# Routing attention and a mixture of experts: first tiles of three experts run ahead, while the last sequence's tokens are placed

## Chip, core and metric

The kernel runs on one core of a Trainium2 chip. The metric is the device time of one execution in microseconds. Before the change the median of three runs is 895.67 us (895.34 to 895.93).

## What is computed

Attention over 4 sequences, 8 heads, 768 positions and 64 channels, in which a query sees only keys of its own cluster of 16, and then a mixture of 8 experts over the 3072 rows of 512 that come out, each row through the one expert that its gate chooses:

```
q_assign, k_assign = argmax(q_n . c_n), argmax(k_n . c_n)
scores = where(q_assign == k_assign, scale * q @ k.T, -1e9)
x = softmax(scores) @ v                       # rows: batch x position, 8 heads side by side
expert_idx = argmax(x @ w_gate)
y[row] = relu(x[row] @ w1[e]) @ w2[e]         # e = expert_idx[row]; w1 512 x 1024, w2 1024 x 512
out = gate_weight * y
```

## The kernel before

**Attention.** Heads are taken in pairs: 16 groups, four to a sequence. A group has 12 units (two halves of the queries by six blocks of keys), and the loop goes in turns of three units, four turns to a group. In each turn `score` makes three score tiles (PSUM tile `sps`, L418 and L421) and their exponentials on ACT (`A`, L423), DVE adds these up (`T`, L426 and L430), and `attend` multiplies the turn before by `v` (`O`, L438). All else is a list of jobs, each set by hand to a turn and to the part of it ahead of or behind `attend`: the turning of q and k for the next group (L344), clusters and their one-hots (`similar`, `assign`, `put`; L358 to L401), `weigh` and `weigh2` (denominators and gate logits, L456 to L489), `x_turn` (rows of x back to tokens, L499 and L502), `gate`, and `keep_rows`, which writes a sequence's rows to `x_rows` in DRAM (L523). The score tiles have three buffers of two PSUM banks (`sps`), the output one bank (`O`), and all the small products one bank with a single buffer (`mps`).

**Placing.** When attention is done, the tokens of all four sequences are placed at once, in an order that a scheduler makes. A scan on DVE ranks the tokens of each partition per expert (`pr`, L613), two small matmuls count across partitions (`cps`, L618), and each token gets a slot: 416 slots for each expert (three tiles of 128 and one of 32), and beyond that a place in spare tiles. To turn slots into lists of tokens, DVE makes one-hots of a slot's row and column (`oh_r`, `oh_c`), POOL multiplies `oh_c` by the token's number (L690), and 24 fp32 matmuls add up `tok_ps` (L698). From it DVE makes the index lists `g_idx` and `s_idx`.

**Experts.** A group is an expert's four tiles, or one spare tile (two of these are always run, further ones in a loop that this data does not enter). `gather` fetches rows by indirect DMAs on POOL (`xg`, L724), `turn_rows` turns them on TensorE and DVE (`tp`, `xgT`, L734 and L735), `layer1` makes 8 blocks of hidden units (`hp`, L743) with the ReLU by turns on DVE (L748) and ACT (L750), `layer2` makes the output tiles (`zp`, L781; the 32-row tile as four quarters, `zq`, and a fold), and `rows_out` scales and scatters them (`zo`, L754; L755). The loop over groups is in written order: layer 1 of a group, turn of the next, layer 2, gather of the one after, fetch of the weights three ahead. Weights have three buffers; those of experts 0 to 2 are fetched during attention, 4 MB each.

PSUM in this stage is laid out anew: three banks for `hp`, two for `tp`, two for `zp`, one for `zq`.

Of the kernel before, what the change touches and what calls it, by code (L numbers as in the profile page):

```python
# [20 lines left out]
NB = 3  # L21
XU = 2
RQ = 32


def in_general(tc, ident, ident_b, first_c, first_e, wpool, q, k, v, centroids, w_gate, w1, w2, out):
# [13 lines left out]
    with tc.tile_pool(name="gen", bufs=1) as sb, tc.tile_pool(name="gen_ps", bufs=1, space=PSUM) as pp:  # L40
# [88 lines left out]
        with tc.For_i(0, N // P, 1) as i:  # L129
# [26 lines left out]
            for e in range(E):  # L156
                we1 = wpool.tile([P, DB, F], F32, name="w1")
                we2 = wpool.tile([P, FB, Dm], F32, name="w2")
# [24 lines left out]
def kernel(  # L183
# [33 lines left out]
    NX = -(-(N - CAP) // P)  # L217
# [7 lines left out]
    wpool = ctx.enter_context(tc.tile_pool(name="weights", bufs=3))  # L225

    def fetch(e):
        w1 = wpool.tile([P, DB, F], F32, name="w1")
        w2 = wpool.tile([P, FB, Dm], F32, name="w2")
        nc.sync.dma_start(out=w1, in_=moe_w1[bass.ds(e, 1)].rearrange("e (a p) f -> p (e a) f", p=P))  # L230
        nc.sync.dma_start(out=w2, in_=moe_w2[bass.ds(e, 1)].rearrange("e (a p) d -> p (e a) d", p=P))
        return w1, w2
# [18 lines left out]

    with ExitStack() as actx:
# [9 lines left out]
        ps_s = actx.enter_context(tc.tile_pool(name="ps_s", bufs=NB, space=PSUM))  # L262
        ps_o = actx.enter_context(tc.tile_pool(name="ps_o", bufs=1, space=PSUM))
        ps_m = actx.enter_context(tc.tile_pool(name="ps_m", bufs=1, space=PSUM))
        actx.enter_context(tc.manual_schedule())
# [35 lines left out]
        ohs = []  # L301
        for i in range(2):
            t = consts.tile([P, 2 * NQ, 2, D], BF16, name=f"oh{i}")
            nc.gpsimd.memset(t, 0.0)
            ohs.append(t)
# [76 lines left out]
        def assign2(g):  # L382
            rank = sims.pop(g)
            top = asg.tile([P, G], F32, name="top")
            nc.vector.tensor_reduce(top, rank, axis=AX, op=ALU.max)
            nc.vector.tensor_tensor(
                ohs[g % 2][:, :, :, 0:C], rank.rearrange("p (t a) c -> p t a c", a=2),
                top.rearrange("p (t a) -> p t a", a=2).unsqueeze(3).to_broadcast([P, 2 * NQ, 2, C]), op=ALU.is_equal,
            )

        def put(g):
            ohT[g] = ohp.tile([P, 2, S], BF16, name="ohT")
            ps = ps_s.tile([P, 2, 512], F32, name="sps").bitcast(BF16)
            for w in range(2):
                for j in range(NQ):
                    nc.tensor.transpose(  # L396
                        ps[:, w, j * P : (j + 1) * P],
                        ohs[g % 2][:, (j % (NQ // 2)) * 4 + w * 2 + j // (NQ // 2)].rearrange("p a c -> p (a c)"), ident_b,
# [92 lines left out]
        def x_turn(g, half):  # L491
# [4 lines left out]
            ps = ps_m.tile([P, 512], F32, name="mps")  # L496
# [41 lines left out]
        NTURN = NG * TG  # L538
        for g in range(NG):
# [10 lines left out]
            at(n + TG + 2, 0, weigh, g)  # L550
            at(n + TG + 2, 1, weigh2, g)
            at(n + TG + 3, 1, x_turn, g, 0)
            at(n + TG + 4, 0, x_turn, g, 1)
            if g % HP == HP - 1:
                at(n + TG + 3, 0, gate, g // HP)
                at(n + TG + 4, 0, keep_rows, g // HP)
# [3 lines left out]
        def early(e):  # L560
            weights[e] = fetch(e)

        for e in range(3):
            at(HP * TG * (e + 1) - 7, 0, early, e)
# [14 lines left out]
    lt_strict = consts.tile([P, P], F32)  # L579
    nc.gpsimd.memset(lt_strict, 1.0)  # L580
    nc.gpsimd.affine_select(
        lt_strict, lt_strict, compare_op=ALU.is_gt, fill=0.0, base=0, pattern=[[1, P]], channel_multiplier=-1,
    )
    ones_sq = consts.tile([P, P], F32)
    nc.gpsimd.memset(ones_sq, 1.0)
    zero_e = consts.tile([P, E], F32)
    nc.gpsimd.memset(zero_e, 0.0)
    keep = consts.tile([P, E, NT], F32)
    nc.gpsimd.memset(keep, 1.0)
    nc.gpsimd.memset(keep[:, :, 0:1], 0.0)  # L590
    b1off = iota("b1off", [P, E], [[(NJ + 1) * P, E]], -1, 0)
    b2off = iota("b2off", [P, E], [[-(NJ + 1) * P, E]], E * (NJ + 1) * P - CAP, 0)
    thr = iota("thr", [P, NX], [[P, NX]], CAP, 0)
    kx = iota("kx", [1, NX], [[1, NX]], 0, 0)
    iota_f = iota("iota_f", [P, P], [[1, P]], 0, 0)
    tokv = iota("tokv", [P, B, NQ], [[S, B], [1, NQ]], 1, NQ)

    g_idx = rte.tile([P, NC], I32)
    s_idx = rte.tile([P, NC], I32)
    xe = rte.tile([1, NX + 2], I32)  # L600

    with tc.tile_pool(name="sm", bufs=1) as sm, tc.tile_pool(name="rps", bufs=1, space=PSUM) as rps:
        sc = sm.tile([P, NT, E], F32)
        nc.vector.tensor_tensor(sc, lg, lmax.unsqueeze(2).to_broadcast([P, NT, E]), op=ALU.is_ge)
        nc.vector.tensor_tensor(sc, sc, first_e[:, None, :].to_broadcast([P, NT, E]), op=ALU.mult)
        mx2 = sm.tile([P, NT], F32)
        nc.vector.reduce_max(mx2, sc, axis=AX)
        sel = sm.tile([P, E, NT], F32)
        nc.vector.tensor_tensor(
            sel.rearrange("p e t -> p t e"), sc, mx2.unsqueeze(2).to_broadcast([P, NT, E]), op=ALU.is_equal,  # L610
        )
        pr = sm.tile([P, E, NT], F32)
        nc.vector.tensor_tensor_scan(  # L613
            pr.rearrange("p e t -> p (e t)"), keep.rearrange("p e t -> p (e t)"), sel.rearrange("p e t -> p (e t)"),
            0.0, op0=ALU.mult, op1=ALU.add,
        )
        cps = rps.tile([P, 2, E], F32, name="cps")
        nc.tensor.matmul(cps[:, 0, :], lhsT=lt_strict, rhs=pr[:, :, NT - 1], start=True, stop=True)  # L618
        nc.tensor.matmul(cps[:, 1, :], lhsT=ones_sq, rhs=pr[:, :, NT - 1], start=True, stop=True)
        cnt = sm.tile([P, 2, E], F32)  # L620
        nc.vector.tensor_copy(cnt, cps)
# [3 lines left out]
            og, cnt[:, 1, :].unsqueeze(2).to_broadcast([P, E, NX]), thr[:, None, :].to_broadcast([P, E, NX]),  # L625
            op=ALU.is_gt,
# [7 lines left out]
        nc.vector.scalar_tensor_tensor(b2, in0=b2, scalar=float(P), in1=b2off, op0=ALU.mult, op1=ALU.add)  # L634
        xk = sm.tile([1, NX, E], F32)
        nc.vector.tensor_tensor(
            xk, ove[0:1, None, :].to_broadcast([1, NX, E]), kx[0:1, :].unsqueeze(2).to_broadcast([1, NX, E]),
            op=ALU.is_le,
        )

# [6 lines left out]
        bps = rps.tile([P, 1], F32, name="bps")  # L647
# [12 lines left out]
        slot = sm.tile([P, E, NT], F32)  # L660
        nc.vector.tensor_tensor(slot, pr, cnt[:, 0, :].unsqueeze(2).to_broadcast([P, E, NT]), op=ALU.add)
        gx = sm.tile([P, E, NT], F32)
        nc.vector.tensor_scalar(gx, slot, scalar1=CAP + 0.5, scalar2=None, op0=ALU.is_ge)
        nc.vector.tensor_tensor(gx, gx, b2.unsqueeze(2).to_broadcast([P, E, NT]), op=ALU.mult)
        nc.vector.tensor_add(slot, slot, gx)
        nc.vector.tensor_tensor(slot, slot, b1off.unsqueeze(2).to_broadcast([P, E, NT]), op=ALU.add)
        nc.vector.tensor_mul(slot, slot, sel)
        sl = sm.tile([P, NT], F32)
        nc.vector.reduce_sum(sl, slot.rearrange("p e t -> p t e"), axis=AX)
        sl_i = sm.tile([P, NT], I32)  # L670
        nc.vector.tensor_copy(sl_i, sl)
        rc_i = sm.tile([P, 2, NT], I32)
        nc.vector.tensor_scalar(rc_i[:, 0, :], sl_i, scalar1=P - 1, scalar2=None, op0=ALU.bitwise_and)
        nc.vector.tensor_scalar(rc_i[:, 1, :], sl_i, scalar1=7, scalar2=None, op0=ALU.arith_shift_right)
        rc = sm.tile([P, 2, NT], F32)
        nc.vector.tensor_copy(rc, rc_i)


        oh_r = sm.tile([P, NT, P], F32)
        oh_c = sm.tile([P, NT, NC], F32)  # L680
        tok_ps = rps.tile([P, NC], F32, name="tok_ps")
        tok = tokv.rearrange("p b j -> p (b j)")
        TH = NT // 4
        for t0 in range(0, NT, TH):
            ts = slice(t0, t0 + TH)
            nc.vector.tensor_tensor(
                oh_c[:, ts, :], iota_f[:, None, :NC].to_broadcast([P, TH, NC]),
                rc[:, 1, ts].unsqueeze(2).to_broadcast([P, TH, NC]), op=ALU.is_equal,
            )
            nc.gpsimd.tensor_tensor(  # L690
                oh_c[:, ts, :], oh_c[:, ts, :], tok[:, ts].unsqueeze(2).to_broadcast([P, TH, NC]), op=ALU.mult,
            )
            nc.vector.tensor_tensor(
                oh_r[:, ts, :], iota_f[:, None, :].to_broadcast([P, TH, P]),
                rc[:, 0, ts].unsqueeze(2).to_broadcast([P, TH, P]), op=ALU.is_equal,
            )
            for t in range(t0, t0 + TH):
                nc.tensor.matmul(tok_ps, lhsT=oh_r[:, t, :], rhs=oh_c[:, t, :], start=(t == 0), stop=(t == NT - 1))  # L698

        tv = sm.tile([P, NC], F32)  # L700
        nc.vector.tensor_scalar(tv, tok_ps, scalar1=-1.0, scalar2=None, op0=ALU.add)
# [101 lines left out]
    with tc.manual_schedule():  # L803
        for i in range(2):
            gather(groups[i])
# [56 lines left out]
```

## Time and profile before

| | |
|---|---|
| median of three runs | 895.67 us |
| the profiled run, its span | 893.96 us, 892.2 us |
| TensorE busy in the span | 843.4 us (95%) |
| DVE, ACT, POOL busy | 309.5, 263.6, 100.6 us |
| from HBM, to HBM | 68.26 MB, 13.68 MB |

Each row of the profile's groups is one line of the kernel on one engine, with its count, its busy time and the mean of one instruction; an fp32 matmul of the program is two records. In tables of windows the clock is the share of full speed that TensorE was granted, and DMA is the mean busy share of the 16 DMA engines. Idle time of an engine is put down to whatever ended it.

### The profile page before, as it was taken

The numbers are of one execution on the slowest core, as the hardware profiler recorded it, in microseconds if no ns is written. First come the engines' busy times: TensorE is split into PE (matmuls) and PEld (weight loads), VectorE is DVE, ScalarE is ACT, GpSimd is POOL, SyncE is SP. The second block draws the span as 40 slices with busy tenths as digits, with TensorE's granted clock in tenths as the row PEclk, the third lists the DMA queues.
The fourth block names the chain that finished last, engine by engine and source line by source line (L and its number), as shares of the span: only waits on it lengthen the run. The fifth ranks groups of instructions, "written<-read, shape, count | busy, mean of one in ns | idle before, by whom it ended". The sixth has DMA issues, their size and how long they took to land.

```text
span 892.2 us, 10340 instructions
## 1 busy us (share of the span) xinstructions
PE 843.4 (95%) x4207; PEld 423.1 (47%) x4207; DVE 309.5 (35%) x523; ACT 263.6 (30%) x404; POOL 100.6 (11%) x153
## 2 busy tenths in 40 slices
PE   4999999999999999999469999999999999999995
PEld 2444454544445444444255454444445454545463
DVE  3555556556555656565621001010102010110000
ACT  3554555455545454554000010101010101001010
POOL 4000000000000000000140020202030201201010
PEclk9999999999999999999759999999999999999998
DMA  6126222272243511200120342424242232333010
GB/s 161 36 55 229 67 54 70 60 240 54 54 125 148 149 29 26 90 1 1 71 78 1 117 146 107 153 107 159 95 154 96 79 141 74 143 118 108 17 36 15
DMA packets 76185, 81.67 MB, mean 92 GB/s; under 512 B 52831, under 2 KB 56927, under 8 KB 75616
## 3 DMA queue, kind: packets, MB, share of 16 engines
q1 hardware_dynamic: 70208, 60.82, 21.5%
q0 software_dynamic: 5248, 20.04, 6.2%
q8 instruction: 36, 0.59, 0.3%
q14 instruction: 21, 0.17, 0.1%
q10 hardware_dynamic: 672, 0.05, 0.0%
HBM read 68.26 MB, written 13.68 MB: 92 GB/s over the span
## 4 chain that ended last, share of the span: by engine, by line
PE 45%; issue 42%; POOL 7%; DVE 3%; ACT 1%; DMA 1%; POOLq 0%; ACTq 0%; DVEq 0%
PE sps L418 14%; PE O L438 14%; PE mps L456 4%; PE sps L421 3%; POOL out_dram L755 3%; POOL xg L724 3%; PE sps L344 2%; PE mps L358 2%; PE mps L499 1%; PE sps L396 1%; PE tok_ps L698 1%; PE mps L369 1%; DVE T L430 1%; ACT A L423 1%; PE mps L470 0%
## 5 line engine op out<-in xcount | busy, mean ns | idle before, releaser
L743 PE MATMUL hp<-xgT,w 128*128 128x416 f32 (+1 forms) x640 | 197.1, 469 | 0.4 <-DVE xgT L735 0.4
L781 PE MATMUL zp<-w,h_sb 128*128 128x512 f32 x416 | 181.0, 594 | 0.0
L423 ACT ACTIVATE A<-sps 128x768 f32<-128x768 f32 x192 | 154.5, 812 | 64.3 <-PE sps L421 63.3
L418 PE MATMUL sps<-qk 64*128 64x384 f32 x768 | 163.8, 501 | 1.0 <-ACT qk L349 1.0
L743 PEld LDWEIGHTS hp<-xgT,w 128*128 128x128 f32 x640 | 111.8, 191 | 87.5 <-issue 86.9
L430 DVE TENSOR_TENSOR T<-T,A 128x768 f32<-128x768 f32 x128 | 122.5, 957 | 49.1 <-ACT A L423 38.8
L438 PE MATMUL O<-A,v_in 128*64 128x384 f32 x768 | 138.0, 495 | 0.0
L748 DVE TENSOR_SCALAR h_sb<-hp 128x416 f32<-128x416 f32 (+1 forms) x40 | 21.3, 532 | 330.5 <-PE hp L743 330.5
L781 PEld LDWEIGHTS zp<-w,h_sb 128*128 128x128 f32 x416 | 78.2, 190 | 101.4 <-issue 101.4
L418 PEld LDWEIGHTS sps<-qk 64*128 64x128 f32 x768 | 68.0, 188 | 36.5 <-issue 31.9
L438 PEld LDWEIGHTS O<-A,v_in 128*64 128x64 f32 x768 | 49.4, 136 | 70.2 <-issue 68.7
L754 ACT ACTIVATE zo<-zp,xg 128x512 f32<-128x512 f32 (+1 forms) x34 | 23.3, 685 | 198.2 <-PE zp L781 196.2
L750 ACT ACTIVATE h_sb<-hp 128x416 f32<-128x416 f32 (+1 forms) x40 | 18.8, 469 | 207.9 <-PE hp L743 207.9
L755 POOL DMA_INDIRECT out_dram<-zo,s_idx x34 | 33.2, 975 | 350.9 <-ACT zo L754 348.5
L421 PE MATMUL sps<-ohT 64*128 64x384 bf16 x384 | 66.2, 324 | 2.0 <-DVE ohT L401 2.0
L426 DVE SCALAR_TENSOR_TENSOR T<-A 128x768 f32<-128x768 f32 x32 | 30.7, 958 | 90.9 <-ACT A L423 90.9
L379 POOL TENSOR_TENSOR sim<-sim,first_c 128x384 f32<-128x384 f32 x16 | 16.0, 997 | 313.7 <-DVE sim L378 313.7
L421 PEld LDWEIGHTS <-ohT 64*128 64x128 bf16 x384 | 22.1, 94 | 26.8 <-DVE ohT L401 5.6
L724 POOL DMA_INDIRECT xg<-x_rows,g_idx x34 | 32.2, 947 | 17.2 <-issue 10.1
L735 DVE COPY xgT<-tp 128x512 f32<-128x512 f32 (+1 forms) x34 | 18.9, 593 | 30.5 <-PE tp L734 30.3
L734 PE MATMUL tp<-ident,xg 128*128 128x128 f32 (+1 forms) x136 | 19.5, 281 | 8.8 <-DMA xg<-x_rows,g_idx 6.3
L446 ACT COPY xT<-O 128x384 f32<-128x384 f32 x32 | 15.4, 481 | 32.2 <-PE O L438 32.2
(152 smaller groups left out, 466.9 us busy)
## 6 DMA issues: line engine op xcount, KB each, us to landing
w<-in_moe_w_dram SPq DMA_DIRECT2D x20, 2048.0 KB, 8.4
x_rows<-x POOLq DMA_DIRECT2D x4, 1548.0 KB, 6.7
q_in<-in_q_dram SPq DMA_DIRECT2D x32, 192.0 KB, 4.4
k_in<-in_k_dram SPq DMA_DIRECT2D x32, 192.0 KB, 4.5
v_in<-in_v_dram SPq DMA_DIRECT2D x16, 384.0 KB, 3.3
xg<-x_rows,g_idx POOLq DMA_INDIRECT x34, 5.2
out_dram<-zo,s_idx POOLq DMA_INDIRECT x34, 2.8
csb<-in_centroids_dram ACTq DMA_DIRECT2D x1, 32.0 KB, 1.7
```

Source lines behind the costliest of these rows:

```text
L418: nc.tensor.matmul(ps[:, a, 0:HS], lhsT=qk[g][r, 1, ks], rhs=qk[g][r, 0, qs], start=True, stop=False)
L421: nc.tensor.matmul(ps[:, a, 0:HS], lhsT=ohT[g][r, 1, ks], rhs=ohT[g][r, 0, qs], start=False, stop=True)
L423: nc.scalar.activation(A[u], ps[:, :, 0:HS], AF.Exp)
L426: nc.vector.scalar_tensor_tensor(T[g, half], in0=A[u - 1], scalar=1e-9 / P, in1=A[u], op0=ALU.add, op1=ALU.add)
L430: nc.vector.tensor_tensor(T[g, half], T[g, half], A[u], op=ALU.add)
L438: nc.tensor.matmul(O[g, half][a * D : (a + 1) * D, 0:HS], lhsT=rows[g, "v"][:, a, j, :], rhs=a_[:, a, :], start=(j == 0), stop=(j == NQ - 1),)
L456: nc.tensor.matmul(ps[half * 32 : (half + 1) * 32, 0:HS], lhsT=one_row[:, i, :] if i < 2 else wg[:, g % HP, :], rhs=t[half][:, i, :] if i ...
L724: nc.gpsimd.indirect_dma_start(out=g["xg"][0:m, j, :], out_offset=None, in_=x_d[:, :], in_offset=bass.IndirectOffsetOnAxis(ap=g["gi"](j)[0 ...
L743: nc.tensor.matmul(hp[:, :cols], lhsT=g["w"][0][:, c, fb * P : (fb + 1) * P], rhs=g["xT"][:, c, :cols], start=(c == 0), stop=(c == DB - 1),)
L754: nc.scalar.activation(zo[0:m], zp[0:m], AF.Copy, scale=g["xg"][0:m, j, Dm : Dm + 1])
L755: ins = nc.gpsimd.indirect_dma_start(out=out[:, :], out_offset=bass.IndirectOffsetOnAxis(ap=g["si"](j)[0:m], axis=0), in_=zo[0:m], in_offs ...
L781: nc.tensor.matmul(zp, lhsT=g["h"][:, fb, j * P : (j + 1) * P], rhs=g["w"][1][:, fb, :], start=(fb == 0), stop=(fb == FB - 1),)
```

## The change

Six parts:

1. **PSUM.** The pools of attention (three `sps` of two banks, `O`, `mps`) live to the end. The expert stage takes all its tiles from `sps` (`wide()`): two blocks of hidden units share one (four each when a group has 128 columns), with DVE's ReLU on one half and ACT's on the other, once per tile; two turned tiles of rows share one. `x_turn` moves from `mps` to `sps`.
2. **Placing in two parts.** The scan, the count and the slots are made for the first three sequences while the last is in attention (`choose`, `count`, `slots1`, `one_hots1`, `tokens1` as jobs of its turns), and for the last one after it (`choose`, `count`, `slots` with the counts of the front as base).
3. **First tiles.** Slots 0 to 127 of experts 0, 1 and 2 hold tokens of the first three sequences only. Their rows are gathered and turned during attention; layer 1 and layer 2 of these three tiles (`first_half`, `layer2`) stand between the steps of the placing. The groups of experts 0 to 2 in the loop have 288 columns in place of 416.
4. **The token search in bf16.** The token's number is split in two (above and below 6 bits), so that the one-hots and both products are bf16: 24 matmuls of 108 columns in place of 24 fp32 ones of 53; POOL makes two products for each quarter in place of one.
5. **Weights.** Those of expert 2 are fetched after the last attend, into room that attention's tiles held.
6. **Order.** Everything is in written order; the constants are made by a job of turn 1. The cluster one-hots have one buffer in place of two. `zc` takes its room from the ring of `zo`.

The core of the diff:

```diff
+    def layer1(g, fbs):
+        cols = sum(g["n"])
+        per = 512 // cols
+        for f0 in range(fbs[0], fbs[1], 2 * per):
+            hp = wide()
...
+            for a in range(2):
...
+                if a == 0:
+                    nc.vector.tensor_relu(dst, src)
+                else:
+                    nc.scalar.activation(dst, src, AF.Relu)
...
+    def turn_rows(g):
+        for j, m in enumerate(g["n"]):
+            if j % 2 == 0:
+                tp = wide().rearrange("p a (c t) -> p a c t", t=P)
+            for c in range(DB):
+                nc.tensor.transpose(tp[:, j % 2, c, 0:m], g["xg"][0:m, j, c * P : (c + 1) * P], ident[0:m, 0:m])
+            nc.vector.tensor_copy(g["xT"][:, :, j * P : j * P + m], tp[:, j % 2, :, 0:m])
...
+    def one_hots(pool, rc, ts, cols, oh_r, oh_c):
+        eq = pool.tile([P, n, w], BF16, name="eq")
...
+        for i in range(2):
+            nc.gpsimd.tensor_tensor(
+                oh_c[:, ts, i, :], eq, hl[:, i, ts].unsqueeze(2).to_broadcast([P, n, w]), op=ALU.mult,
+            )
...
+        n = (NG - HP) * TG
+        at(n + 3, 1, choose, pl, front)
+        at(n + 4, 1, count, front)
+        at(n + 5, 0, slots1)
+        at(n + 5, 1, one_hots1, 0)
+        at(n + 6, 0, one_hots1, 1)
+        at(n + 7, 0, tokens1)
+        for i in range(NP):
+            at(n + 7, 1, gather1, i)
+            at(n + 13, i % 2, turn_rows1, i)
...
+        n = NG * TG
+        at(n + 1, 0, first_half, 0)
+        at(n + 1, 0, weigh, NG - 1)
+        at(n + 1, 0, layer2, groups1[0])
+        at(n + 1, 1, weigh2, NG - 1)
+        at(n + 1, 1, gate, B - 1)
+        at(n + 1, 1, x_turn, NG - 1, 0)
+        at(n + 1, 1, x_turn, NG - 1, 1)
+        at(n + 1, 1, keep_rows, B - 1)
...
-        for e in range(3):
+        for e in range(2):
             at(HP * TG * (e + 1) - 7, 0, early, e)
...
+    weights[2] = fetch(2, 2)
+    with tc.tile_pool(name="sm", bufs=1) as sm:
+        choose(sm, back)
+        first_half(1)
+        count(back)
...
+        for t0 in range(0, NT, TQ):
+            one_hots(sm, rc, slice(t0, t0 + TQ), k_["iota"], oh_r, oh_c)
+        layer2(groups1[1])
+        tokens(tok_ps, oh_r, oh_c, NT)
+        indices(sm, tok_ps, NC, g_idx, s_idx)
...
+        first_half(2)
+        bps = ps_m.tile([P, 512], F32, name="mps")[:, 0:1]
...
+    for i in range(2):
+        gather_of(groups[i])
+    layer2(groups1[2])
+    turn_of(groups[0])
```

## The prediction

> **What bounds the kernel now.** I read first the table of windows (duration; busy time of each engine; granted clock; DMA share), cut at the ends of the stages:
>
> ```profile
> core 0: us, PE busy (x) PEld busy (x) DVE busy (x) ACT busy (x) POOL busy (x), PEclk, DMA share, GB/s
> 20.00:401.50 381.50, 377.70 (x2601) 183.87 (x2597) 225.57 (x347) 203.82 (x303) 19.85 (x36) 1.00 0.29 87
> 427.70:465.50 37.80, 19.58 (x91) 15.76 (x91) 20.20 (x62) 1.19 (x3) 12.77 (x13) 0.59 0.22 75
> 514.40:562.80 48.40, 48.05 (x147) 23.35 (x146) 5.24 (x9) 4.81 (x8) 7.69 (x8) 1.00 0.34 122
> ```
>
> TensorE is busy 99% of attention and of an expert. The hole is between: from the last attend (427.7) to the first `hp` matmul (465.5) are 37.8 us at clock 0.59, with little but placing tokens. Then TensorE's waits in that window:
>
> ```profile
> PE tok_ps L698 <- POOL oh_c L690: 7.0, 1, 7.0
> PE tp L734 <- DMA xg<-x_rows,g_idx: 6.3, 3, 5.6
> ```
>
> It is one chain, DVE to POOL to TensorE to DVE to gather. Last the timeline, for the prices:
>
> ```profile
> 475.65 0.59 DVE L748 TENSOR_SCALAR h_sb<-hp 128x416 f32<-128x416 f32 x1 [4.99 <-PE hp L743]
> 481.24 0.59 DVE L748 TENSOR_SCALAR h_sb<-hp 128x416 f32<-128x416 f32 x1 [5.00 <-PE hp L743]
> ...
> 869.96 0.29 DVE L748 TENSOR_SCALAR h_sb<-hp 128x128 f32<-128x128 f32 x1 [1.44 <-PE hp L743]
> 871.74 0.29 DVE L748 TENSOR_SCALAR h_sb<-hp 128x128 f32<-128x128 f32 x1 [1.50 <-PE hp L743]
> ```
>
> ```profile
> 489.41 1.04 PE L734 MATMUL tp<-ident,xg 128*128 128x128 f32 x8
> 490.80 1.03 PE L734 MATMUL tp<-ident,xg 128*128 128x128 f32 x8 [0.35 <-DVE xgT L735]
> 491.76 0.64 PE L772 MATMUL zq<-w,h_sb 128*32 128x512 f32 x4
> ```
>
> ```profile
> 443.15 1.21 POOL L690 TENSOR_TENSOR oh_c<-oh_c,tokv 128x318 f32<-128x318 f32 x1 [5.21 <-DVE oh_c L686]
> 444.78 1.37 POOL L690 TENSOR_TENSOR oh_c<-oh_c,tokv 128x318 f32<-128x318 f32 x1 [0.42 <-DVE oh_c L686]
> ```
>
> Two ReLUs on one engine are 16 passes apart (each fp32 matmul is two records): 5.59/16 = 0.349 us a pass at 416 columns, 1.78/16 = 0.111 at 128; on the line between, 0.244 at 288. ACT's `zo` are 6.87 us apart (500.78, 507.65): layer 2 costs 6.9 per tile. So 128 rows alone through an expert cost 64 x 0.111 = 7.1, plus 6.9, and cutting 416 into 128 and 288 is nearly free. The turn of a group's rows takes 489.41 to 491.76 = 2.35 us, with one wait.
>
> **What the skill says.** "TensorE: Matmul & The Clock Gate", Part 1: the clock is halved after an idle window and comes back after some 3.4 us of work. The trace agrees: the first `hp` weight loads stand 0.69 us apart until 468.4, then 0.35; expert 0's layer 1 took 23.9 (465.51 to 489.41), not 22.4. "SBUF — State Buffer", Who interferes with whom: a DVE operation with two SBUF inputs contends with a POOL one that reads SBUF. It agrees: DVE L686 took 0.49 alone, 1.00 beside POOL L690. "PSUM — Partial Sum Buffer", PSUM bank collisions: the scheduler orders engines that touch one bank and quadrant. In the built program the order is by PSUM tile, two banks here: ACT's ReLU waits for DVE's of the same tile, and transposes into the second half wait for the copy out of the first. No run yet shows its price.
>
> **Part by part.** Sums are on the profiled span, 892.2; its run took 893.96 and the three runs have median 895.67, so I carry the difference over.
>
> *Start, -0.7.* One `oh` memset of 1.35 us (two take 2.69) goes. DVE's two `cn` operations stretch to 1.58 us beside them, and TensorE's first transpose waits for `cn` until 7.78. At most -1.3; +0.5 if the constants, now after the first `sim` product, get in DVE's way. The constants' 30 small POOL operations end long before group 1 needs POOL. I take half.
>
> *Attention, +4.1.* x_turn into `sps`: its copies land before the third score after it (556 ns at 356.0 to 356.6; the slot is wanted at 357.9): 0. Added: count, 4 passes, 0.35. DVE's choice (5 operations of 144, 1.9) fits in the 3.7 us it idles. slots1 (11 operations, 3.3) and the one-hots (0.2 + 1.4, twice) don't: DVE idles 3.7 in that turn, then runs late to the end of group 13. I followed its queue: assign's `oh` is still in time for put (before at 372.08, wanted at 373.4, now about 1.5 later); weigh2's `ls` copy, behind the second one-hot, holds the only `mps` bank 1.0 longer than tokens1 can wait; 18 bf16 matmuls take 1.3 (73 ns each, as L396); behind indices1 the third score of group 14 waits 0.5. Turning three tiles: 1.6. One stall at the end (0.65, L499 on `mps`) goes. Bounds +3 and +8. The three gathers (0.95 each on POOL) are hidden by five turns of attention.
>
> *From the last attend to the first `hp` of the loop.* T = 0 at that attend; F = first half, Z = layer 2 of a first tile. TensorE: F0 to 7.1; weigh 2.1, to 9.2; Z0 to 16.1; weigh2 and x_turn 1.3, to 17.4; F1 to 24.5. DVE does ls, gate, x and choose from 16.6 to about 22, behind Z0, and its next, the ReLU of F1 (0.7), comes before `cnt`: 25.6. From `cnt` to POOL's first product were 5.7 us (437.44 to 443.15); now more operations on smaller tiles, 6.1: 31.7. Z1 lies beside this. POOL has eight products in place of four, two per quarter, and `eq` has one buffer, so DVE's next `eq` (0.49, and 0.35 of handing over) stands between quarters. Price: the first of a pair beside DVE's `oh_r` 1.33, as L690; the second alone 0.85, L379's 0.997 for 384 scaled to 324. 4 x 2.2 + 3 x 0.84 = 11.3, to 43.0. The bounds are 9 (the skill's page "GPSIMD Engine Reference", 3.1, 2.6 cycles an element at 1.2 GHz: estimate 0.70 each) and 13.5 (1.37 each); a bf16 product on POOL no row shows. Last six token matmuls, cold: 44.0. In the hole ahead of that TensorE idles some 9 us, so F2 pays a cold start, 1.8: 52.9. Z2 waits for DVE's ReLU, 0.9, since a 128-column first half now fills one tile: 60.7. The turn: 3.1, hp at 63.8.
> The third weights are asked for at T = 0 on SP's queue, ahead of xe's loads, and take 2 x 8.4 = 17 us: before 44. The gathers must wait too: `moe_x` takes the place of `sm`, so the first gather waits for the last `xe` write, which waits for bps behind F2. That is 54.8; then 0.96 to POOL's start and 3.6 to the transpose (455.94, 456.90, 460.49 before), the third tile 2.95 later: 62.3, just before it is wanted (62.6). Sum: 63.8 - 37.8 = **+26.0**.
>
> *Taken out of the loop.* Layer 1 of three experts 3 x 64 x (0.349 - 0.244) = 20.3; layer 2 3 x 6.87 = 20.6; expert 0's cold start 1.5; turns of three tiles for four 0.3: **-42.7**.
>
> *Given back in the loop.* In a turn of four tiles, as ordered in the build: the last DVE ReLU now waits for its whole pair (0.2 + 0.6), then copy 0 (0.7, to 1.5), then tile 1 (0.5), tile 2 (0.5), copies 1 and 2 to 3.5, tile 3: 3.85 in place of 2.35. Experts 3 to 7: 5 x 1.5 = **+7.5** (bounds 0, if tile 1 need not wait, and 9). Expert 7's end and the two spare tiles wait for ReLUs now in one piece: 0.8 + 0.4 + 0.9 = **+2.1**. `zo` and `zc` in one ring: ACT's third `zo` waits for fold, 0.5, hidden by the next layer 1. Weights for experts 3 to 7 start two experts ahead of their use (69 us against 17): 0.
>
> Sum: -0.7 + 4.1 + 26.0 - 42.7 + 7.5 + 2.1 = **-3.7**, and 895.7 - 3.7 = **892.0**.
>
> **The rivals.** *A, POOL becomes the bound of the search.* Eight products, and nothing on TensorE to fill the wait. For it: four already took TensorE 7.0 us of waiting, and mixed bf16 and fp32 is new. Against it: half of them run with DVE still. Each 0.1 us more per product is 0.8; from a mean of 1.75 (mine is 1.1) the kernel is slower by over 0.2%; at 1.95 it is 895.7 - 3.7 + 6.8 = 898.8.
> *B, the gathers end last.* They have 0.3 us to spare. If POOL starts on `xe` 3 us later than I have it, TensorE waits 3 us for the rows at 62: 895. For it: a chain of six small DVE operations across F2's end. Against it: Z2 covers 7 us.
> *C, the turns are not serialised,* and POOL is at its lower bound: -7.5 - 2 more, 882.5. For it: banks differ. Against it: the waits stand in the build.
>
> **How the numbers follow.** A measurement can tell about 0.2% (1.8 us) from no change. Forecast 0.55 (its own terms spread over 887 to 896: 0.44 faster, 0.08 same, 0.03 slower); A 0.20 (0.18 slower, 0.02 same); B 0.12 (0.08 same, 0.04 faster); C 0.13 (faster). Faster 0.61, same 0.18, slower 0.21. The range reaches to A's value and most of the way to C's: 885.5 to 898.8.
>
> **What would show it.** Right: the last attend at about 431; the loop's first `hp` about 64 us behind it; POOL's last product about 43 behind; a clock near 1.0 until T = 33 and 0.5 again at F2; turns of four tiles 3.9 long with a wait on the copy of `xgT`; layer 1 of experts 0 to 2 near 15.6. Wrong step by step: an attend ending after 434 (attention mis-sized), products over 1.5 (A), a transposes' wait on the DMA (B), turns under 3 (C). If the loop's first `hp` is under 55 behind the attend, the chain's order is not the one I followed.

## The result, and the profile after

The changed kernel takes 890.30 us (median of four executions, 890.06 to 893.70) against 895.73 before; the ratio is 0.9949, 95% interval 0.9925 to 0.9973. Eight more executions of it, beside thirteen of the kernel before on one chip, gave 892.04 against 894.84, ratio 0.9964 (0.9951 to 0.9978). So it is faster by 0.4 to 0.5%; the forecast was 892.0, or 0.41%. The twelve executions of the changed kernel together have median 891.0 and spread over 3.7 us.

One caution ahead of the traces: the profiled execution of before was among its shorter ones (893.96 us, span 892.2), the profiled one of after is the longest of its twelve (893.70, span 891.7). The two traces therefore differ by 0.5 us only, and the ledger further down is made for that pair, not for the medians.

The table of windows of the changed kernel (duration, busy time by engine, clock, DMA share): attention, then from the last attend to the loop's first `hp`, then one expert of four tiles:

```profile
20.00:401.00 381.00, 376.38 (x2595) 183.51 (x2593) 230.93 (x373) 201.46 (x300) 28.35 (x49) 1.00 0.28 78
431.04:493.03 61.99, 52.36 (x305) 37.66 (x304) 21.24 (x72) 5.05 (x9) 17.48 (x19) 0.92 0.33 121
703.40:753.33 49.93, 48.14 (x148) 23.36 (x147) 5.24 (x9) 4.81 (x8) 7.68 (x8) 1.00 0.33 118
```

The stretch behind attention is 62.0 us long instead of 37.8, but TensorE works in 52.4 of it (19.6 before) at clock 0.92 (0.59). An expert of four tiles is 49.9 us instead of 48.4, with the same 48 us of TensorE work: 1.5 us of new waiting. TensorE's waits over the whole run name it (who waited for whom: us in total, times, longest us; the first line is the kernel before):

```profile
PE tp L734 <- DVE xgT L735: 2.4, 7, 0.3
PE sps L280 <- DVE xgT L281: 11.2, 13, 0.9
PE mps L469 <- POOL oh_c L459: 7.0, 4, 2.2
```

Before, the turns' wait on the copy of `xgT` was 2.4 us in seven pieces; now it is 11.2 in thirteen. The wait on POOL's products is 7.0 us as before, but in four pieces. TensorE's timeline over the end of that stretch (start, duration, what; in brackets the idle time before it and what ended it):

```profile
456.63 7.13 PE L336 MATMUL sps<-w,h 128*128 128x512 f32 x16 [0.43 <-DVE h L300]
464.63 0.45 PE L469 MATMUL mps<-oh_c,oh_r 128*128 128x108 bf16 x6 [0.86 <-POOL oh_c L459]
...
472.63 0.70 PE L469 MATMUL mps<-oh_c,oh_r 128*128 128x108 bf16 x6 [1.97 <-POOL oh_c L459]
473.12 9.02 PE L292 MATMUL sps<-xT,w 128*128 128x128 f32 x64
...
491.35 1.02 PE L280 MATMUL sps<-ident,xg 128*128 128x128 f32 x8 [0.78 <-DVE xgT L281]
493.03 2.64 PE L292 MATMUL sps<-xgT,w 128*128 128x288 f32 x6 [0.67 <-issue]
```

Z1, four quarters of token products that each wait for POOL, F2 at 9.02 us where F0 and F1 took 7.3, Z2 and the turn: the order that was forecast. The timeline gives POOL's pace (a quarter's two products as one row, then each by itself, and the DVE comparison beside the first):

```profile
467.85 2.06 POOL L459 TENSOR_TENSOR oh_c<-eq,hl 128x324 bf16<-128x324 bf16 x2 [0.61 <-DVE eq L454]
467.85 1.37 POOL L459 TENSOR_TENSOR oh_c<-eq,hl 128x324 bf16<-128x324 bf16 x1 [0.61 <-DVE eq L454]
469.19 0.72 POOL L459 TENSOR_TENSOR oh_c<-eq,hl 128x324 bf16<-128x324 bf16 x1
467.69 0.95 DVE L462 TENSOR_TENSOR oh_r<-iota_f,rc 128x768 bf16<-128x768 f32 x1
```

Two products take 2.06 us and the handing over from DVE 0.61, a period of 2.67 a quarter. The two are not alike: the first, beside DVE's `oh_r`, takes 1.37 us, the second, alone, 0.72. Last, two turns of four tiles of the same execution, into experts 4 and 6:

```profile
622.74 0.60 PE L280 MATMUL sps<-ident,xg 128*128 128x128 f32 x4
624.18 1.09 PE L280 MATMUL sps<-ident,xg 128*128 128x128 f32 x8 [0.84 <-DVE xgT L281]
626.22 0.43 PE L280 MATMUL sps<-ident,xg 32*128 32x32 f32 x4 [0.94 <-DVE xgT L281]
626.58 3.53 PE L325 MATMUL sps<-w,h_sb 128*32 128x512 f32 x16
...
729.70 1.92 PE L325 MATMUL sps<-w,h_sb 128*32 128x512 f32 x16
```

The turn takes 3.84 us (622.74 to 626.58) with two waits, where it took 2.35 with one. Then look at the sixteen `zq` products behind it: 3.53 us after the first turn, 1.92 after the other, the same instructions. The windows show why: TensorE's granted clock is 0.50 from 627 to 630 us. That was in no forecast, and the experiments had to explain it.

### The profile page after: what moved, and what is told of

The parts are those of the page before. It is cut to its first block, busy times and chain, and to the rows that moved or that the text cites. A ratio compares the mean times of both kernels' runs of the same rounds, so it can differ in the third digit from the quotient of the medians.

```text
span 891.7 us, 10764 instructions
## 1 busy us (share of the span) xinstructions
PE 842.9 (95%) x4397; PEld 438.8 (49%) x4397; DVE 315.8 (35%) x559; ACT 263.4 (30%) x401; POOL 107.6 (12%) x165
## 4 chain that ended last, share of the span: by engine, by line
PE 45%; issue 39%; POOL 7%; DVE 5%; ACT 1%; DMA 0%; POOLq 0%; ACTq 0%; DVEq 0%
PE sps L652 14%; PE O L672 13%; PE mps L690 3%; PE sps L655 3%; POOL out_dram L307 3%; POOL xg L270 3%; PE sps L292 3%; PE sps L578 3%; DVE T L664 2%; PE mps L592 1%; PE sps L733 1%; PE sps L630 1%; POOL oh_c L459 1%; PE mps L603 1%; PE sps L336 1%
## 5 line engine op out<-in xcount | busy, mean ns | idle before, releaser
L292 PE MATMUL sps<-xgT,w 128*128 128x416 f32 (+2 forms) x640 | 176.8, 437 | 0.7 <-issue 0.7
L336 PE MATMUL sps<-w,h_sb 128*128 128x512 f32 x368 | 160.6, 595 | 1.3 <-DVE h_sb L300 0.9
L292 PEld LDWEIGHTS sps<-xgT,w 128*128 128x128 f32 x640 | 112.2, 192 | 67.7 <-issue 50.6
L300 DVE TENSOR_SCALAR h_sb<-sps 128x416 f32<-128x416 f32 (+2 forms) x34 | 18.7, 550 | 317.9 <-PE sps L292 317.9
L336 PEld LDWEIGHTS sps<-w,h_sb 128*128 128x128 f32 x368 | 69.1, 190 | 93.1 <-issue 91.2
L306 ACT ACTIVATE zo<-sps,xg 128x512 f32<-128x512 f32 (+1 forms) x34 | 23.3, 685 | 206.1 <-PE sps L336 197.1
L302 ACT ACTIVATE h_sb<-sps 128x416 f32<-128x416 f32 (+2 forms) x34 | 16.5, 484 | 166.5 <-DVE h_sb L300 166.5
L280 PE MATMUL sps<-ident,xg 128*128 128x128 f32 (+1 forms) x136 | 18.5, 267 | 11.2 <-DVE xgT L281 11.2
L690 PE MATMUL mps<-T,one_row 128*32 128x384 f32 x128 | 23.8, 492 | 0.0
```

The costliest lines, as they stand in the source:

```text
L292: nc.tensor.matmul(o, lhsT=g["w"][0][:, c, fb * P : (fb + 1) * P], rhs=g["xT"][:, c, :cols], start=(c == 0), stop=(c == DB - 1),)
L336: nc.tensor.matmul(zp, lhsT=g["h"][:, fb, j * P : (j + 1) * P], rhs=g["w"][1][:, fb, :], start=(fb == 0), stop=(fb == FB - 1),)
L690: nc.tensor.matmul(ps[half * 32 : (half + 1) * 32, 0:HS], lhsT=one_row[:, i, :] if i < 2 else wg[:, g % HP, :], rhs=t[half][:, i, :] if i ...
```

## The experiments

All times of an experiment stand beside the kernel before on the same chip (894.84 us for the changed kernel again, turns apart, ReLUs apart and two buffers of `eq`; 894.29 for turns filled; 894.89 for the other four).

**The changed kernel again.**

> The changed kernel once more, nothing edited, for a second profile of it. Clock theory: the profiled execution (893.7 us) was 3.4 us longer than the three others (890.06 to 890.36) because TensorE's clock was halved twice for some 1.7 us each, behind the two waits of a turn of four tiles (the sixteen L325 products took 3.53 and 3.44 us there, 1.92 elsewhere). Then the runs here differ by whole steps of about 1.7 us, most of them near 890.2, and the profile shows one L325 group of 3.5 us for each step. Rival: the 3.4 us lie somewhere else (attention, a transfer, the tail), and then two profiles of equal time differ in single stages by amounts that are no multiple of 1.7.

Measured: 890.00 to 893.60 us over eight executions. The profiled one (893.60) again has the two long `zq` groups, 3.61 and 3.35 us, at the same two experts. Those two make up 3.1 us. The steps aren't whole, though: executions of 890.83, 891.24 and 892.85 us lie between, and only two of eight are within 0.2 of 890. The clock theory survives as to the place, not as to equal steps; granted clock and span go together (888.1 us at 0.986, 891.7 at 0.982).

**Turns apart.**

```
-            if j % 2 == 0:
-                tp = wide().rearrange("p a (c t) -> p a c t", t=P)
+            tp = wide().rearrange("p a (c t) -> p a c t", t=P)
...
-                nc.tensor.transpose(tp[:, j % 2, c, 0:m], g["xg"][0:m, j, c * P : (c + 1) * P], ident[0:m, 0:m])
-            nc.vector.tensor_copy(g["xT"][:, :, j * P : j * P + m], tp[:, j % 2, :, 0:m])
+                nc.tensor.transpose(tp[:, 0, c, 0:m], g["xg"][0:m, j, c * P : (c + 1) * P], ident[0:m, 0:m])
+            nc.vector.tensor_copy(g["xT"][:, :, j * P : j * P + m], tp[:, 0, :, 0:m])
```

> Each tile of rows is turned in a PSUM tile of its own; the rest is as changed. Theory (transposes into the second half of a PSUM tile wait for the copy out of its first half): the waits of 0.8 and 0.95 go, a turn of four tiles takes 2.4 instead of 3.8 us, five of them give 7, the three shorter ones 0.5 each at most; 882 to 884 us, and with the waits gone no halved clock behind a turn. Rival 1 (the waits are DVE's pace, one copy after the other, whatever the tile): turns stay at 3.8 and the time at 890. Rival 2 (the third tile now takes the slot of the last layer-1 tile and waits for ACT's ReLU instead): turns of 3.0 to 3.3, 886 to 888 us.

Measured: 878.00 us (876.62 to 878.93), ratio to before 0.9809 (0.9796 to 0.9822): 13 us less than the changed kernel, nearly twice the forecast. The same turn:

```profile
617.24 1.04 PE L279 MATMUL sps<-ident,xg 128*128 128x128 f32 x8
618.64 1.02 PE L279 MATMUL sps<-ident,xg 128*128 128x128 f32 x8 [0.36 <-ACT h_sb L301]
619.58 1.92 PE L324 MATMUL sps<-w,h_sb 128*32 128x512 f32 x16
```

It is 2.34 us long, and the wait that is left is the third tile's, for a ReLU of ACT (the second rival, at 0.36 us instead of 1). Four turns lost 1.5 each, the one into expert 3 lost 1.66 (3.77 to 2.11), those of three tiles 0.8 each (2.33 to 1.52), and the first 0.9 (3.07 to 2.18): 10.2. The rest is the clock: no `zq` group is over 1.93 us but the one behind the spare tile's turn (2.22, as in the changed kernel, at full clock), and expert 0's layer 1 took 15.6 instead of 17.3.

The Trainium skill's page "PSUM — Partial Sum Buffer", PSUM bank collisions, says that the compiler's scheduler orders engines by bank and quadrant. That isn't all that happened here: the two tiles of rows lay in different banks of one PSUM tile, and were ordered all the same; with a PSUM tile each, they are not. In this kernel the unit of ordering is the PSUM tile, and a wait for it costs 0.8 to 0.95 us.

**Turns filled.** To part the turn's length from its gaps:

```
             if j % 2 == 0:
                 tp = wide().rearrange("p a (c t) -> p a c t", t=P)
+            elif g["rows"] == N:
+                fill = ps_m.tile([P, 512], F32, name="mps")
+                for c in range(6 if m == P else 8):
+                    nc.tensor.transpose(fill[:, c % 4 * P : (c % 4 + 1) * P], ident, ident)
```

> The changed kernel with its turns as they are, and TensorE given idle work in their waits: six transposes of the identity (0.9 us) ahead of the second tile of a loop turn and eight (1.2 us) ahead of the fourth, into a PSUM tile that nothing reads. The turns stay as long as they were or get 0.3 longer. Clock theory (a turn's gaps, not the turn's length, drop TensorE's clock for 1.7 us behind some of them, and that spreads the executions of the changed kernel over 890.0 to 893.7): no group of L325 takes over 2 us, expert 0's layer 1 takes 15.6 instead of 17.3, the granted clock is 0.988 or more, the executions agree within 1 us and lie at 888 to 890 us. Rival (the halved clock behind the turns comes from the load on the chip or from the weights that arrive then): L325 groups of 3.5 stay, and the time is 891 to 894.

Measured: 888.79 us (888.35 to 889.05), ratio 0.9937 (0.9923 to 0.9951). The turn into expert 4:

```profile
621.62 0.82 PE L282 MATMUL mps<-ident 128*128 128x128 f32 x6
622.63 1.09 PE L284 MATMUL sps<-ident,xg 128*128 128x128 f32 x8 [0.19 <-DVE xgT L285]
623.55 1.04 PE L282 MATMUL mps<-ident 128*128 128x128 f32 x8
...
625.02 1.92 PE L329 MATMUL sps<-w,h_sb 128*32 128x512 f32 x16
```

The turn is as long as it was (3.84), nothing useful was added, and the kernel is 2.2 us shorter than the median of the changed one (on another chip; by the ratios to the kernel before, 0.9937 against 0.9949 and 0.9964, it is 1.1 to 2.4): every `zq` group behind a turn of three or four tiles is 1.92, expert 0's layer 1 is 15.6, and five executions agree within 0.7 us instead of 3.7. So the gaps halve the clock, not the load and not the weights that land then. (The mean clock came out at 0.986, not the 0.988 that was expected: F2's cold start and the start of the run remain.) The Trainium skill's page "TensorE: Matmul & The Clock Gate", Part 1, speaks of an idle window of about 3.4 us and of a window that runs free of the kernel. The second fits the runs, since only some turns are hit and the same kernel varies. As to the first the measurement decides: here no single gap is over 0.95 us; two of them, 1.8 us in a turn of 3.84, are enough in some turns.

Which turns are hit can be read from the traces. In the changed kernel's trace the clock is halved for 6.83 us at the start, for 10.24 in the search and F2, and for 3.41 behind each turn that was hit, and 6.83 and 10.24 are two and three times 3.41; so its profile can be cut at such steps. The turns into experts 4, 5 and 6, each with the stretch that holds the gaps and the one behind it:

```profile
core 0: us, PE busy (x) PEld busy (x) DVE busy (x) ACT busy (x) POOL busy (x), PEclk, DMA share, GB/s
623.33:626.75 3.42, 1.63 (x17) 1.33 (x20) 2.15 (x5) 0.52 (x1) 0.00 (x0) 1.00 0.68 243
626.75:630.16 3.41, 3.41 (x17) 0.56 (x9) 0.23 (x2) 0.00 (x0) 0.00 (x0) 0.50 0.91 371
674.53:677.95 3.42, 1.63 (x15) 1.16 (x13) 2.46 (x4) 0.52 (x1) 0.00 (x0) 1.00 0.63 196
677.95:681.36 3.41, 3.41 (x20) 0.84 (x19) 0.29 (x1) 0.00 (x0) 0.00 (x0) 0.50 1.00 411
725.73:729.15 3.42, 1.81 (x13) 1.21 (x11) 2.35 (x4) 0.52 (x1) 0.00 (x0) 1.00 0.48 154
729.15:732.56 3.41, 3.23 (x23) 1.27 (x24) 1.11 (x3) 0.00 (x0) 0.00 (x0) 1.00 1.02 422
```

Both gaps lie in one stretch at the first two turns, which leaves TensorE busy for 1.63 us of it (as the profile counts), and the next stretch has half the clock. At the third a gap reaches over the step; TensorE is busy for 1.81 us, and the clock stays, though the DMAs behind it are as busy as behind the others. In the six traces with long `zq` groups all twelve follow a stretch with 1.62 to 1.70 us of work; the turns of four tiles that left 1.75 us or more weren't hit. That is no share for all work: at the turn ahead of the loop a stretch with 1.97 us (490.21 to 493.63) was followed by a halved one.

**ReLUs apart.**

```
-        for f0 in range(fbs[0], fbs[1], 2 * per):
+        for f0 in range(fbs[0], fbs[1], per):
             hp = wide()
...
-            for a in range(2):
...
-                if a == 0:
-                    nc.vector.tensor_relu(dst, src)
...
+            if f0 // per % 2 == 0:
+                nc.vector.tensor_relu(dst, src)
```

> Each layer-1 result has a PSUM tile of one bank, DVE and ACT in turn, instead of two banks with a ReLU of each; the turn stays as changed. Theory (DVE's last ReLU waits for the whole pair of banks and ACT's for DVE's): the last two ReLUs end 0.6 to 0.8 earlier; the waits of layer 2 for h go in the first tiles (0.43 and 0.74 on the path) and at the two spare tiles (0.47 and 0.86), and the turns get 0.3 to 0.6 shorter: -2 for the waits and -1.5 to -3 for the turns, 886 to 887 us. Rival (three tiles of one bank hold TensorE back, where six banks did not): layer 1 at 416 columns takes over 22.6 us per expert, and the time is 890 or more.

Measured: 887.44 us (886.31 to 888.32), ratio 0.9921 (0.9908 to 0.9934). The waits of layer 2 for `h` are gone, 0.43 and 0.74 in the first tiles, 0.47 and 0.86 in the spare ones; expert 0 starts warm (15.6), for 1.7 more, which isn't the edit's doing: the turn ahead of it has the same two waits as in the changed kernel, 0.78 and 0.67, and the next run is warm there too. Layer 1 at 416 columns stays at 22.45, so the rival falls. The other half of the theory failed: a turn of four tiles still takes 3.78 us. The late ReLU cost 0.06 us there, not 0.3 to 0.6.

**Two buffers of eq.** The one-hot of columns is allocated with `bufs=2`; nothing else.

> The one-hot of columns gets a second buffer, so DVE writes the next quarter's while POOL multiplies; the rest is as changed. Theory (POOL's eight products with DVE's hand-over between them set the end of the search, and all behind it follows): the period of a quarter falls from 2.67 to 2.06, the last product ends 1.8 us earlier, the loop's first hp is 60.2 instead of 62.0 behind the last attend, 888.5 us. Rival 1 (something else is next at once, the gathers or the third weights): the last product ends 1.8 earlier and the first hp moves by less than 0.5. Rival 2 (DVE and POOL contend for SBUF): the products get longer, 1.2 instead of 1.03 each, and half of the gain is lost.

Measured: 891.31 us (889.88 to 891.63), ratio 0.9959 (0.9947 to 0.9971): not to be told from the changed kernel. The hand-over is gone, and POOL's eight products run without a gap, but they got longer:

```profile
462.72 8.97 POOL L459 TENSOR_TENSOR oh_c<-eq,hl 128x324 bf16<-128x324 bf16 x8 [9.71 <-DVE eq L454]
```

That is 1.12 us each in the mean instead of 1.03: with two buffers DVE's comparisons run beside both products of a pair, which take 1.44 and 0.97 instead of 1.37 and 0.72; only the last one, with none beside it, still takes 0.72. The last product ends 1.0 us earlier behind the last attend, not 1.8 (rival 2 had this right). F2 then took 9.41 instead of 9.02 and kept 0.4 of it. The loop's first `hp` came 61.4 behind the last attend instead of 62.0.

**F2 ahead of the token products.**

```
         layer2(groups1[1])
...
+        first_half(2)
         tok_ps = ps_m.tile([P, 512], F32, name="mps")[:, 0 : 2 * NC]
         tokens(tok_ps, oh_r, oh_c, NT)
+        bps = wide()[:, 0, 0:1]
+        nc.tensor.matmul(bps, lhsT=ones_sq, rhs=bad[:, 2:3], start=True, stop=True)
         indices(sm, tok_ps, NC, g_idx, s_idx)
```

> The first half of the third first tile (F2) runs ahead of the token products instead of behind them, and the small operations on xk, fit and bad ahead of it; bps follows the token products in a two-bank PSUM tile. Theory (TensorE waits 7.0 us for POOL's products with work at hand, and F2 then runs at half clock): F2 lies in that wait and takes 7.3 instead of 9.0; the token products end at 475 instead of 473, the gathers start at about 478 instead of 485 and their rows, not TensorE, set the loop's first hp, 55 to 56 behind the last attend instead of 62.0; 884 to 886 us. Rival 1 (POOL's chain and the hand-over to the gathers are the bound, whatever TensorE does): 60 to 62 and 889 or more. Rival 2 (the third weights are not there at 464): TensorE waits for them and the kernel is slower.

Measured: 880.45 us (880.09 to 882.49), ratio 0.9840 (0.9827 to 0.9853): 10.5 less than the changed kernel, and 4 less than expected, from F2 moved with a few small operations around it.

```profile
463.00 7.31 PE L292 MATMUL sps<-xT,w 128*128 128x128 f32 x64
...
472.30 0.45 PE L469 MATMUL mps<-oh_c,oh_r 128*128 128x108 bf16 x6 [1.12 <-POOL oh_c L459]
...
473.54 7.11 PE L336 MATMUL sps<-w,h 128*128 128x512 f32 x16 [0.26 <-issue]
...
481.87 1.02 PE L280 MATMUL sps<-ident,xg 128*128 128x128 f32 x8 [0.79 <-DMA xg<-x_rows,g_idx]
```

F2 runs in the wait for POOL and warm (7.3 instead of 9.0). The first `hp` is at 483.56, 53.1 behind the last attend instead of 62.0 (8.9 of the 10.5), and expert 0's layer 1 takes 15.6 instead of 17.3 (1.7). One part of the expectation didn't hold: the rows hardly bound it, since the 0.79 ahead of the second tile is no longer than the wait for the copy elsewhere. F2 at 32.6 behind the last attend didn't wait for the third weights, so their later fetch costs nothing even there.

**The bf16 search alone**, put into the kernel before: `eq`, two POOL products per quarter into `oh_c[:, ts, i, :]`, 24 bf16 products.

> The kernel before with the bf16 token search alone: eq, two POOL products per quarter, 24 bf16 products on TensorE; everything else as before. Theory (POOL's eight products take what TensorE's fp32 products took): four quarters of 2.67 from 15.4 behind the last attend, the last six products 0.7, end at 26.8 to 27.0; before it was 27.2; one more index operation. No change: 894 to 896 us. Rival 1 (the 10.5 us of fp32 products were the bound and fall away): the first hp comes 6 to 7 earlier, 888 us. Rival 2 (mixed operands slow POOL beside DVE): 898.

Measured: 895.17 us (22 executions, 893.79 to 896.64), ratio 1.0007 (1.0000 to 1.0014): no change. TensorE's token products:

```profile
453.90 0.69 PE L706 MATMUL tok_ps<-oh_c,oh_r 128*128 128x106 bf16 x6 [1.31 <-POOL oh_c L698]
```

Their 10.48 us are down to 4 times 0.69, but the last ends at 454.6, 26.4 behind the last attend (428.2), where it was 27.3: POOL's second product per quarter took the place of what TensorE saved. The 0.9 us that are left went into expert 0's layer 1, 24.9 instead of 23.9 behind the colder stretch.

**Without the first tiles.** All of F0 to F2, Z0 to Z2, and their search, gathers and turns in attention are left out; the eight experts have four tiles each in the loop (`j0 = 0`).

> The changed kernel without its first tiles: no one-hots, token search, gathers and turns for them in attention, none of F0 to F2 and Z0 to Z2, all eight experts with four tiles in the loop; early choice and slots of three sequences, bf16 search, PSUM tiles and late third weights as changed. Theory (first tiles take 41 us out of the loop and put 24 into the hole, the turns cost 1.5 each): hole 38 to 39 us as before, attention 3 shorter, loop 41 plus 4.5 to 6 for three more turns of four tiles longer: 905 to 910 us, so the first tiles are worth 15 to 19 and the rest of the change costs 10 to 14. Rival (the placing ahead of the hole and the bf16 search already shorten the hole by 5 or more): 898 to 902.

Measured: 912.67 us (911.78 to 915.82), ratio 1.0207 (1.0189 to 1.0226). That is 3 us over the expected range: the first tiles are worth some 21 us and everything else in the change costs 18, more on both sides than expected. In its trace (span 912.5, 20.3 over before) seven turns of four tiles cost 10.4, three long `zq` groups (3.62, 3.32 and 3.40) 4.7, the stretch behind attention 2.8 (40.6 us), a colder expert 0 1.0, the spare tiles 2.2, and attention is 1.0 shorter: 20.1.

**Together.** Turns apart, ReLUs apart, two buffers of `eq`, the first halves' ReLUs all on ACT, `count` in the middle of F1, and F2 cut in two:

```
+        first_half(1, 0)
         count(back)
+        first_half(1, 1)
...
         layer2(groups1[1])
+        first_half(2, 0)
+        bps = wide()[:, 0, 0:1]
...
         tokens(tok_ps, oh_r, oh_c, NT)
+        first_half(2, 1)
...
         indices(sm, tok_ps, NC, g_idx, s_idx)
```

> The changed kernel with everything that seems to hold it back mended at once: a PSUM tile per turned tile, one bank per layer-1 result, two buffers of eq; the first halves' ReLUs all on ACT; count in the middle of F1; F2 in two halves around the token products, bps ahead of these, xe's operations ahead of the indices. Theory: 878 (turns apart) less 2 for the waits on h, less 9 to 10 for the hole (first hp 52 behind the last attend instead of 61.6, set by TensorE's own work): 866 to 868 us. Rival (the rows come late, 0.96 + 3.6 + 2.9 us behind the last index): first hp 55 behind, 869 to 871. A second rival (three one-bank tiles are too few for turns and layer 1 together): turns over 2.5 and 872 or more.

Measured: 864.82 us (864.01 to 865.27), ratio to before 0.9667 (0.9654 to 0.9680), 1 us under the expected range; the profiled execution has clock 0.995.

```profile
468.53 0.45 PE L467 MATMUL mps<-oh_c,oh_r 128*128 128x108 bf16 x6 [1.16 <-DVE xe_f L939]
...
481.50 0.75 PE L291 MATMUL sps<-xgT,w 128*128 128x288 f32 x2 [0.78 <-DVE xgT L280]
```

The first `hp` is 51.9 behind the last attend (429.64), and TensorE waits 1.2 us in the search where it waited 7.0. Turns of four tiles take 1.98. It beats both kernels, the changed one by 26 us; the single steps (13, 10.5, 3.6 and nothing) sum to 27, with the clock's part counted more than once.

## Why the prediction was right, and where it was not

The ledger of the two profiled executions, cut at the same instructions in both (us):

| term | forecast | measured |
|---|---|---|
| start and attention, to the last attend | +3.4 | +3.3 (427.7 to 431.0) |
| last attend to the loop's first `hp` | +26.0 | +24.2 (37.8 to 62.0) |
| layer 1 of experts 0 to 2, with the cold start | -21.8 | -20.3 (68.8 to 48.5) |
| layer 2 of experts 0 to 2 | -20.6 | -20.6 (70.9 to 50.3) |
| seven turns | +7.2 | +7.5 (16.4 to 23.9) |
| halved clock behind turns | none | +3.1 (3.46 and 3.37 for 1.85) |
| expert 7's layer 2 and the spare tiles | +2.1 | +2.2 (63.8 to 66.0) |
| sum | -3.7 | -0.6 (spans: -0.5) |

*The mechanism was right.* The gain is the first tiles in a stretch where TensorE idled; it is nearly all paid back by the longer chain there and by the turns. Without the first tiles the kernel is 18 us slower than before; the bf16 search by itself is worth nothing, because POOL's eight products take over what TensorE's products gave up. The chain's steps came within 2 us each: POOL's first product at 31.6 behind the last attend (31.7 forecast), its last end at 41.5 (43.0), the first `hp` at 62.0 (63.8).

*The POOL term was high.* A pair took 2.06 instead of 2.2 (1.37 and 0.72, where 1.33 and 0.85 were forecast), the handing over 0.61 instead of 0.84: 1.3 of the 1.8 us. Rival A needed a mean product of 1.75 (by its own sum that is 1.5 us slower, 0.17%); it was 1.03. The estimate of 0.70 for a product alone, from which the lower bound was made, was met: 0.72. But eight of these and three hand-overs of 0.84 are 8.1 us, not the 9 that the forecast gave as its bound, and C would then lie at 881.3.

*The turns were right in size, partly for a wrong reason.* 3.85 was forecast and 3.84 came. But the sum had 0.8 us for the last ReLU waiting for its pair; with that gone a turn is 0.06 shorter. The waits are those for the copies out of the first half of the tile, as the turns apart show. The forecast also measured the damage against 2.35, the turn of before; apart, three tiles take 1.5, so the changed kernel's seven turns cost 9.4, not 7.5, against what they could be.

*Start and attention were right by luck.* The forecast had -0.7 for the start and +4.1 for the placing's first part and the turns of the first tiles. At the last attend of group 12, ahead of all that, the changed kernel is 0.5 behind (330.98 to 331.45), and the rest adds 2.9. The clock can have had a part in the first: it was halved for 3.4 us at the start before (17.9 to 21.3) and for 6.8 after (15.8 to 22.6). Without the first tiles the last attend comes 1.0 earlier than before, so it is they, not the placing, that cost time there.

*The step that failed is the clock.* "Expert 0's cold start 1.5" was booked as gone, since F2 and Z2 keep TensorE busy up to the turn. It stayed (17.28 instead of 15.6): behind the waits of the turn, 0.78 and 0.67, the clock was halved again from 494 to 497. (It isn't so in every run: with ReLUs apart and with two buffers of `eq` the same waits left the clock whole.) And no term said that turns with two waits do the same in the loop; it is +3.1 in this trace, and less in shorter executions. Filling the gaps removes both. In this trace the two are 4.6 us (1.5 and 3.1), more than the whole gain that was forecast; the shorter chain gave 1.8 back. Over all twelve executions the clock costs some 2.2 us in the median (891.0 against 888.8 with filled turns). That the forecast's 892.0 lies so close to the measured medians is partly luck: 1.8 us too much for the chain and some 2 us forgotten for the clock nearly cancel.

*The rivals.* B (gathers last) didn't happen: the first gather started at 53.7 behind the last attend, and TensorE never waited for rows. C had the turns free of serialising as a case worth 882.5; made true by a PSUM tile per turned tile, without its part on POOL, it gives 878.

*Not tried:* fetching the third weights as early as before, for which attention's buffers leave no room; and POOL's products with no DVE operation beside any of them.

## What to carry to other kernels

When two steps share one tile of PSUM, or one buffer, count what the second must wait for, per turn and times the number of turns, and look at what follows: on TensorE two gaps of 0.8 to 0.95 us close together halved the clock for the next 3.4 us in some turns, so that 1.8 us of waiting cost 1.6 us more. When work is brought in to fill a wait, put it in program order where the wait is: the same F2, behind the token products or ahead of them, is 10.5 us apart. A faster form on one engine (bf16 on TensorE) gives nothing while another engine prepares its operands at the same pace.

## What the runs showed of the hardware

- TensorE's clock fell to half behind turns whose gaps were 0.84 and 0.94 us in a span of 3.84, in one to three of the turns of an execution, and the next 1.85 us of work took 3.25 to 3.55; with the same turns filled with idle transposes no turn of that trace was hit, and all five executions had clock 0.986.
- In the loop the halved clock came in stretches of 3.41 us, and the stretch before each tells which turns were hit: all twelve, in six traces, had 1.62 to 1.70 us of TensorE's work in it, and the turns of four tiles with 1.75 us or more were spared. At the turn ahead of the loop the line lay higher (1.97 us was followed by a halved stretch).
- A program's spread can be such clock steps: 890.0 to 893.7 us with the gaps, 888.35 to 889.05 without.
- A product of 128 x 324 in bf16 on POOL took 0.72 us alone and 1.37 beside DVE's comparison into `oh_r`; the fp32 products of 128 x 318 before, with DVE beside them too, took 1.36 or 1.37 but for the first (1.21). So what set the price was DVE beside the product; beside DVE bf16 saved nothing, and an fp32 product alone is not on record.
- DVE pays as well: with two buffers its comparison into `eq` took 1.02 us beside POOL instead of 0.50, that into `oh_r` 1.48 instead of 0.95.
